# Batch 0 of a linear-attention and gated-FFN kernel: sums of phi(k) by products of their own, kv straight from the loaded v, phi of q's second part in two pieces

## The chip, the cores and the metric

The kernel runs on one core of a Trainium2 chip. The metric is the device time of one execution in microseconds (us). The kernel before takes 297.05 us (median of three runs, 296.93 to 297.34). A verdict of faster or slower needs 2%, which is 5.9 us here; the change is far smaller than that, so most of this document is about where a saved microsecond went, read from traces. All results compared are of fast runs (a run is called slow when it lies over 1.5% above the fastest of its kernel).

Engines: PE multiplies matrices (PEld is its weight load), DVE and ACT work elementwise, POOL issues most loads, SP the stores.

## The reference, cut to what matters

```python
def phi(x): return np.where(x > 0, x, np.exp(x) - 1.0) + 1.0
q_p, k_p = phi(q), phi(k)                        # 8 batches, 8 heads, 576 tokens, 64 wide
kv  = np.einsum('bhsd,bhse->bhde', k_p, v)
z   = np.sum(k_p, axis=2)                        # the "sums"
num = np.einsum('bhsd,bhde->bhse', q_p, kv)
den = np.einsum('bhsd,bhd->bhs', q_p, z)[..., None] + 1e-06
x   = (num / den)  # -> [4608, 512]
h   = x @ w_in                                   # 512 -> 2048
out = (h * sigmoid(beta * h)) @ w_out            # 2048 -> 512
```

## The kernel before: the parts that matter

PE works batch by batch: h of batch b, then y of batch b, with the attention of batch b+1 between the y products. Batch 0 has nothing to hide behind: its k, q, v must land, phi, kv, numerator, division and transpose run in a chain, and only then can the first h product start. "The plan" of a phase is the list of such work put between its products. While PE would idle there, `warm(n)` issues n filler products of 512 columns whose result nobody reads.

In kv, a column of ones beside v gives the sums of phi(k). So v is first copied by DVE into a wider tile, in two halves of the heads:

```python
    load_nine(v9, v, h1=2)
    load_nine(v9, v, h0=2)
...
    def v_copy0(h0, h1):
        nc.vector.tensor_copy(
            va9[:, :, h0:h1, 0:D].rearrange("p j h d -> p h j d"), v9[:, h0:h1])

    def kv_mm0(a, kvp):
        for j in range(N9):
            for g in range(2):
                ... nc.tensor.matmul(kvp[g][:, m0 : m0 + 2 * (D + 1)],
                    st["p0"][1][gs, j, 2 * a : 2 * a + 2, :],
                    va9[gs, j, 2 * a : 2 * a + 2, 0 : D + 1],
                    start=(j == 0), stop=(j == N9 - 1), skip_group_check=True)
```

The loads are issued by POOL in this order, and land one after another: k, q, v of batch 0, four blocks of w_in, two of w_out's four blocks, k and q of batch 1, w_out's third block, **v of batch 1**, w_out's last block. After the h phase of batch 0, y starts, and after ten of its sixteen blocks PE does batch 1's kv:

```python
    exp_(1, 1); exp_(1, 0); silu_table()
    relu(1, 1); relu(1, 0); w_out_scale(2)
    phi(1, 1)
    v_copy(1)          # DVE waits for v of batch 1
    phi(1, 0)
    y_phase_wide(0, {
        ...
        9: [F(kv_mm, 1), F(kv_evac, 1), F(w_out_scale, 3)],
        10: [F(q_trans, 1, 0, 1, wide=True), F(q_trans, 1, 2, 3, wide=True)],
```

Of the kernel before, what the change touches and what calls it, by code (L numbers as in the profile page):

```python
# [10 lines left out]
BF16 = mybir.dt.bfloat16  # L11
# [5 lines left out]
def kernel(  # L17
# [10 lines left out]
    nc = tc.nc  # L28

    B, H, S, D = q.shape  # L30
    DM = H * D
    DFF = moe_w_in.shape[1]
    P = 128
# [4 lines left out]
    TAIL = S - MAIN  # L38
    NT = NJ + 1
    EA = D + 2  # L40
# [5 lines left out]
    consts = ctx.enter_context(tc.tile_pool(name="consts", bufs=1))  # L46
# [4 lines left out]
    def mm_bank(shape, dtype=F32):  # L51
        return mmps.tile(shape, dtype, tag="mm", name="mm")

    def att_banks(dtype=F32):

        n = 512 if dtype == F32 else 1024
        return attps.tile([P, 2, n], dtype, tag="att", name="att")

    NX = 3
    HH = H // 2  # L60
    xqk = [consts.tile([P, 2, H, NT, D], BF16, name=f"xqk{i}") for i in range(NX)]
    vraw = [consts.tile([P, H, NT, D], BF16, name=f"vraw{i}") for i in range(2)]
    vaug = [consts.tile([P, NT, H, EA], BF16, name=f"vaug{i}") for i in range(2)]
# [51 lines left out]
    N9 = S // TAIL  # L115

    def nine(a, spec):

        names = " ".join(spec)
        flat = a.rearrange("p a b c -> p (a b c)")  # L120
        size = {"h": HH, "j": N9, "d": EA if a is vaug[0] else D}
        n = size["h"] * size["j"] * size["d"]
        return flat[:, 0:n].rearrange(f"p ({names}) -> p {names}", **size)

    q9 = nine(xqk[0][:, 0], "hjd")
    k9 = nine(xqk[0][:, 1], "hjd")
    v9 = nine(vraw[0], "hjd")
    va9 = nine(vaug[0], "jhd")

    def load_nine(dst, src, h0=0, h1=HH, j0=0, j1=N9):  # L130
        for g in range(2):
            nc.gpsimd.dma_start(  # L132
                out=dst[g * TAIL : (g + 1) * TAIL, h0:h1, j0:j1, :].rearrange(
                    "p h j d -> p h (j d)"
                ),
                in_=src[0, g * HH + h0 : g * HH + h1, :, :]
                .rearrange("h (p j) d -> p h j d", j=N9)[:, :, j0:j1, :]
                .rearrange("p h j d -> p h (j d)"),
            )
# [13 lines left out]
    load_nine(q9, q, j1=4)  # L153
    make_identity(nc, identity)
    make_identity(nc, ident16)
    load_nine(v9, v, h1=2)
    load_nine(v9, v, h0=2)
    load_nine(q9, q, j0=4)
    for i in range(4):
        nc.gpsimd.dma_start(out=w_in_sb[i], in_=w_in_v[:, :, i * 512 : (i + 1) * 512])  # L160
# [15 lines left out]
    def set_ones(i):  # L176
        nc.vector.memset(vaug[i][:, :, :, D : D + 2], 1.0)
        nc.vector.memset(vaug[i][TAIL:P, NJ, :, D : D + 2], 0.0)

    nc.vector.memset(va9[:, :, :, D : D + 2], 1.0)  # L180
    set_ones(1)



# [31 lines left out]
    st = {}  # L216

    def by_dma(b):
        return b >= DMA_T
# [48 lines left out]
    def phi0(a, j0, j1):  # L268
        nc.vector.tensor_tensor(
            st["p0"][a][:, j0:j1], st["r0", a][:, j0:j1], st["e0", a][:, j0:j1], ALU.min  # L270
        )

    def q_trans0(t, banks, c0):


        for jj in range(2 if t < NJ else 1):
            for a in range(2):
                for g in range(2):
                    gs = slice(g * TAIL, (g + 1) * TAIL)
                    m0 = c0 + a * P + jj * TAIL  # L280
                    nc.tensor.matmul(
                        banks[:, g, m0 : m0 + TAIL],
                        st["p0"][0][gs, 2 * t + jj, 2 * a : 2 * a + 2, :],
                        identity[gs, gs],
                        is_transpose=True, start=True, stop=True, skip_group_check=True,
                    )

    def q_out0(t, banks, c0, dve):
        n = rows(t)
        src = banks[:, :, c0 : c0 + 2 * P].rearrange("p g (a n) -> p g a n", a=2)  # L290
        dst = st[0, "qT"][:, t].rearrange("p (g a) n -> p g a n", g=2)
        copy(dst[:, :, :, :n], src[:, :, :, :n], dve)

    def v_copy0(h0, h1):
        nc.vector.tensor_copy(
            va9[:, :, h0:h1, 0:D].rearrange("p j h d -> p h j d"), v9[:, h0:h1]
        )

    def kv_mm0(a, kvp):
        for j in range(N9):  # L300
            for g in range(2):
                gs = slice(g * TAIL, (g + 1) * TAIL)
                m0 = a * 2 * (D + 1)
                nc.tensor.matmul(
                    kvp[g][:, m0 : m0 + 2 * (D + 1)],
                    st["p0"][1][gs, j, 2 * a : 2 * a + 2, :],
                    va9[gs, j, 2 * a : 2 * a + 2, 0 : D + 1],
                    start=(j == 0), stop=(j == N9 - 1), skip_group_check=True,
                )

    def kv_evac0(kvp):
        for g in range(2):
            for i in range(2):
                gs = slice(i * D, (i + 1) * D)
                copy(
                    kv_bd[0][g][gs, :, i, :],
                    kvp[g][gs, 0 : 4 * (D + 1)].rearrange(
                        "p (a i e) -> p a i e", a=2, i=2
                    )[:, :, i, :],
                    g == 0,  # L320
                )
# [32 lines left out]
    def rows(t):  # L354
        return P if t < NJ else TAIL
# [7 lines left out]
    def copy(dst, src, dve):  # L363
        if dve:
            nc.vector.tensor_copy(dst, src)  # L365
        else:
            nc.scalar.activation(dst, src, ACTF.Copy)
# [33 lines left out]
    def num_norm(b, t):  # L401
        n = rows(t)
        den = work.tile([P, 2, 4], F32, tag="den", name="den")
        rden = work.tile([P, 2, 4], F32, tag="rden", name="rden")
        xs = work.tile([P, 2, 4, D], BF16, tag="xs", name="xs", bufs=4)
        st[b, "xs", t] = xs
        nv = st[b, "n", t][:n, :, 0 : 4 * (D + 1)].rearrange("p a (h e) -> p a h e", h=4)
        nc.vector.tensor_scalar(den[:n], nv[:, :, :, D], 1e-6, None, ALU.add)  # L408
        nc.vector.reciprocal(rden[:n], den[:n])  # L409
        nc.vector.tensor_mul(  # L410
            xs[:n], nv[:, :, :, 0:D], rden[:n, :, :, None].to_broadcast([n, 2, 4, D])
        )
        if by_dma(b):
            nc.sync.dma_start_transpose(
                out=x_dst(b, t), in_=xs.rearrange("p a h d -> p (a h d)")[:n]
            )

    def x_dst(b, t):
        if t < NJ:
            return xT[b % 3][:, t]  # L420
        return xT_tail[:, :, b * TAIL : (b + 1) * TAIL]

    def x_trans(b, t, wide=False, dve=False):
        n = rows(t)
        xv = st[b, "xs", t].rearrange("p a h d -> p (a h d)")
        tp = tr_bank(wide)[:, 0 : KC * P].rearrange("p (c n) -> p c n", c=KC)
        for p in range(KC):
            nc.tensor.matmul(
                tp[:, p, :n], xv[:n, p * P : (p + 1) * P], identity[:n, :n],
                is_transpose=True, start=True, stop=True, skip_group_check=True,  # L430
            )
        copy(x_dst(b, t), tp[:, :, :n], dve)
# [132 lines left out]
    def warm(n):  # L565
        for _ in range(n):
            nc.tensor.matmul(  # L567
                st["warm"], g_sb[0][:, FC - 1, 0:P], g_sb[0][:, FC - 1, :],
                start=True, stop=True, skip_group_check=True,
            )  # L570

    def silu_table():
        nc.scalar.activation(small[:, 1:2], small[:, 0:1], ACTF.Silu)

    def F(f, *a, **k):
        return lambda: f(*a, **k)
# [17 lines left out]
    relu0(0, 0, 4)  # L594
    phi0(1, 5, N9)
    phi0(0, 0, 4)
    v_copy0(0, 2)
    qb = att_banks(BF16)
    q_trans0(0, qb, 0)
    q_trans0(1, qb, 256)  # L600
    kvp = [mm_bank([P, 512]) for _ in range(2)]
    kv_mm0(0, kvp)
    q_out0(0, qb, 0, False)
    q_out0(1, qb, 256, False)
    warm(1)
    v_copy0(2, HH)
    kv_mm0(1, kvp)
    kv_evac0(kvp)
    st["warm"] = mm_bank([P, 512])
    warm(1)  # L610
# [3 lines left out]
    relu0(0, 4, N9)  # L614
    silu_table()
    num_norm(0, 0)
    warm(4)
    x_trans(0, 0, dve=True)
    phi0(0, 4, N9)
    num_norm(0, 1)  # L620


    def q_tail0():
        qb3 = att_banks(BF16)
        q_trans0(4, qb3, 0)
        q_out0(4, qb3, 0, True)

    load_w_out(2)
    load_v(1)
    load_w_out(3)  # L630

    def tidy0():
        set_ones(0)
        clear_tail(0)
        nc.vector.memset(vraw[0][TAIL:P, :, NJ, :], 0.0)

    def q_second():
        qb2 = att_banks(BF16)
        q_trans0(2, qb2, 0)
        q_trans0(3, qb2, 256)  # L640
        q_out0(2, qb2, 0, False)
        st["qb2"] = qb2

    h_phase(
        0, xT[0],
# [1 line left out]
        + [(ff, 0, 2) for ff in range(4, 8)] + [(ff, 2, 4) for ff in range(8)]  # L647
        + [(ff, 0, 4) for ff in range(8, 12)],
        {
            1: [F(q_second)],  # L650
            3: [F(x_trans, 0, 1, dve=True), F(num_mm, 0, 2), F(num_norm, 0, 2),
                lambda: q_out0(3, st["qb2"], 256, False)],
            5: [F(num_mm, 0, 3), F(num_norm, 0, 3)],
            6: [F(q_tail0)],
            7: [F(x_trans, 0, 2)],
            9: [F(x_trans, 0, 3)],
            10: [F(num_mm, 0, 4), F(num_norm, 0, 4), F(tidy0)],
            14: [F(x_trans, 0, 4)],
            17: [F(w_out_scale, 0), F(w_out_scale, 1)],
        },  # L660
    )
# [114 lines left out]
```

## Time and profile before

| place in the trace before | us |
|---|---|
| kv's products of batch 0 end | 13.50 |
| first block of w_in has landed (the weight load that waited for it) | 16.37 |
| first h product | 16.77 |
| first y product | 34.27 |
| copy of batch 1's v, start and end | 41.90, 42.91 |
| batch 1's kv products start | 43.00 |
| last copy of the result | 291.44 |

The page's first line gives the busy times of the engines. PE idles 10.7 us in all, and 4.7 us of them lie in the first 20 us (busy 15.3 there) and 3.9 us after its last product (291.41 of 295.27).

```profile
PE 284.6 (96%) x1876; PEld 144.7 (49%) x1897; DVE 126.1 (43%) x267; ACT 175.0 (59%) x232; POOL 52.8 (18%) x72
```

A row of a timeline reads: start, length, engine, line of the program, operation, output and inputs, shape, how many; in brackets how long the engine stood idle before it and what ended that.

### The profile page before, as it was taken

How to read it: one execution, taken by the hardware profiler on the slowest of the kernel's cores; microseconds unless marked ns; L12 is line 12 of the kernel's file. 1: busy time of each engine (PE TensorE's matmuls, PEld its weight loads, DVE VectorE, ACT ScalarE, POOL GpSimd, SP SyncE). 2: the span in 40 equal slices, each digit the busy share in tenths (PEclk: the TensorE clock that was granted, in tenths of full speed). 3: DMA queues.
4: the chain of work that ended last, by engine and by line, in shares of the span. 5: the costliest groups of instructions: out<-in, count | busy, mean ns of one | idle time of the engine just before them, and what ended most of it. 6: DMA issues, size and time to landing. Idle time of an engine off the chain costs nothing.

```text
span 295.3 us, 4721 instructions
## 1 busy us (share of the span) xinstructions
PE 284.6 (96%) x1876; PEld 144.7 (49%) x1897; DVE 126.1 (43%) x267; ACT 175.0 (59%) x232; POOL 52.8 (18%) x72
## 2 busy tenths in 40 slices
PE   8689999999999999999999999999999999999994
PEld 3467445644555544445444544454445444444443
DVE  4776488504772174616461646154715400110012
ACT  2788786889988780778087907790770077018500
POOL 8925575444006000330020000000000000000000
PEclk9999999999999999999999999999999999999999
DMA  7999999999939933798357355024502400020033
GB/s 106 190 207 344 256 273 192 256 194 190 162 140 154 178 93 98 133 175 149 98 125 82 80 109 125 2 71 115 124 2 72 118 36 0 36 94 15 0 72 72
DMA packets 69206, 36.43 MB, mean 123 GB/s; under 512 B 37808, under 2 KB 63680, under 8 KB 69184
## 3 DMA queue, kind: packets, MB, share of 16 engines
q0 software_dynamic: 38400, 20.45, 47.5%
q1 hardware_dynamic: 30624, 15.55, 20.5%
q8 instruction: 15, 0.25, 0.3%
q10 hardware_dynamic: 160, 0.13, 0.2%
q14 instruction: 7, 0.06, 0.1%
HBM read 36.71 MB, written 9.44 MB: 156 GB/s over the span
## 4 chain that ended last, share of the span: by engine, by line
PE 72%; DMA 14%; POOL 5%; ACT 4%; issue 3%; DVE 1%; POOLq 0%; ACTq 0%; DVEq 0%
PE mm L500 33%; PE mm L448 33%; DMA vraw<-in_v_dram 9%; DMA xT<-in_moe_w_out_dram 5%; PE att L394 3%; ACT e L228 2%; POOL xqk L132 1%; PE att L339 1%; PE mm L532 1%; POOL w_in L160 1%; ACT L228 1%; POOL vraw L132 1%; POOL vraw L72 1%; ACT g L440 1%; DVE qk_p L241 0%
## 5 line engine op out<-in xcount | busy, mean ns | idle before, releaser
L440 ACT ACTIVATE g<-mm,beta_c 128x512 bf16<-128x512 f32 (+2 forms) x156 | 97.4, 632 | 88.4 <-PE mm L448 88.2
L500 PE MATMUL mm<-w_out,g 128*128 128x512 bf16 x541 | 127.2, 379 | 1.2 <-issue 0.3
L448 PE MATMUL mm<-xT,w_in 128*128 128x512 bf16 (+2 forms) x560 | 108.0, 349 | 0.8 <-DVE xT L365 0.8
L448 PEld LDWEIGHTS <-w_in 128*128 128x128 bf16 x656 | 62.1, 98 | 61.7 <-issue 0.7
L500 PEld LDWEIGHTS <-g 128*128 128x128 bf16 x560 | 52.8, 98 | 57.3
L510 DVE COPY y_sb<-mm 128x512 f32<-128x512 f32 x27 | 18.7, 691 | 70.6 <-PE mm L500 68.4
L228 ACT ACTIVATE e<-xqk 128x2560 bf16<-128x2560 bf16 x14 | 31.9, 2329 | 0.1
L410 DVE TENSOR_TENSOR xs<-att,rden 128x512 bf16<-128x512 f32 (+1 forms) x40 | 27.6, 689 | 1.4
L241 DVE TENSOR_TENSOR qk_p<-r,e 128x2560 bf16<-128x2560 bf16 x14 | 20.8, 1489 | 13.1 <-ACT e L228 12.4
L350 DVE CAST kv_bd<-att 64x130 bf16<-64x130 f32 x28 | 8.2, 292 | 34.5 <-PE att L339 34.1
L72 POOL DMA_DIRECT2D vraw<-in_v_dram x7 | 6.4, 910 | 75.6 <-DVE vaug L365 71.0
L408 DVE TENSOR_SCALAR den<-att 128x8 f32<-128x8 f32 (+1 forms) x40 | 6.4, 161 | 26.9 <-PE att L394 26.7
L394 PEld LDWEIGHTS <-q_pT 128*128 128x128 bf16 (+1 forms) x160 | 11.7, 100 | 10.4 <-DVE xs L410 2.1
L394 PE MATMUL att<-kv_bd,q_pT 128*128 128x130 bf16 (+1 forms) x160 | 15.8, 221 | 0.6 <-DVE kv_bd L365 0.3
L448 PE MATMUL mm<-xT_tail,w_in 128*128 128x512 bf16 x63 | 13.9, 379 | 0.1
L236 DVE TENSOR_SCALAR r<-xqk 128x2560 bf16<-128x2560 bf16 x14 | 11.6, 830 | 3.8 <-DMA xqk<-in_q_dram 2.3
L567 PE MATMUL mm<-g 128*128 128x512 bf16 x35 | 9.9, 436 | 1.2 <-DVE g L144 1.2
L228 ACT ACT_TABLE_LOAD x7 | 9.0, 1283 | 0.1
L72 POOL DMA_DIRECT2D xqk<-in_k_dram x7 | 6.9, 981 | 11.1 <-ACT e L228 4.6
L409 DVE RECIPROCAL rden<-den 128x8 f32<-128x8 f32 (+1 forms) x40 | 8.1, 201 | 1.4
L72 POOL DMA_DIRECT2D xqk<-in_q_dram x7 | 6.5, 922 | 6.6 <-DMA xqk<-in_k_dram 2.5
L76 POOL DMA_DIRECT2D xqk<-in_k_dram x7 | 7.0, 1000 | 2.6 <-DMA w_in<-in_moe_w_in_dram 2.6
(72 smaller groups left out, 141.7 us busy)
## 6 DMA issues: line engine op xcount, KB each, us to landing
out_dram<-y_sb SPq DMA_DIRECT2D x28, 256.0 KB, 2.3
xqk<-in_k_dram POOLq DMA_DIRECT2D x7, 512.0 KB, 10.7
xqk<-in_q_dram POOLq DMA_DIRECT2D x7, 512.0 KB, 11.3
vraw<-in_v_dram POOLq DMA_DIRECT2D x7, 512.0 KB, 11.7
w_in<-in_moe_w_in_dram POOLq DMA_DIRECT2D x4, 512.0 KB, 11.4
g<-in_moe_w_out_dram POOLq DMA_DIRECT2D x4, 512.0 KB, 10.9
out_dram<-y_sb SPq DMA_DIRECT2D x14, 128.0 KB, 5.2
xqk<-in_moe_w_out_dram POOLq DMA_DIRECT2D x2, 512.0 KB, 14.5
```

What stands on the lines that cost most here:

```text
L72: eng.dma_start(out=dst[:, :, 0:NJ, :].rearrange("p h j d -> p h (j d)"), in_=src[b, :, 0:MAIN, :].rearrange("h (p j) d -> p h (j d)", j=NJ),)
L228: nc.scalar.activation(st[b, "e", a][:, h0:h1], xqk[b % NX][:, a, h0:h1], ACTF.Exp)
L236: nc.vector.tensor_scalar(st[b, "r", a][:, h0:h1], xqk[b % NX][:, a, h0:h1], 0.0, 1.0, ALU.max, ALU.add)
L241: nc.vector.tensor_tensor(st[b, "p"][:, a].rearrange("p j (h d) -> p h j d", h=H)[:, h0:h1], st[b, "r", a][:, h0:h1], st[b, "e", a][:, h0: ...
L350: nc.vector.tensor_copy(kv_bd[b % 2][i][gs, :, g, :], st[b, "kvp"][gs, 2 * i : 2 * i + 2, :])
L394: nc.tensor.matmul(nps[:n, p // 2, c0 : c0 + 2 * (D + 1)], st[b, "qT"][:, t, p, :n], kv_bd[b % 2][p // 2][:, p % 2], start=True, stop=True ...
L410: nc.vector.tensor_mul(xs[:n], nv[:, :, :, 0:D], rden[:n, :, :, None].to_broadcast([n, 2, 4, D]))
L440: nc.scalar.activation(g_sb[b % 2][:, ff, c0:c1], hp[:, c0:c1], ACTF.Silu, scale=beta_c[:, ff : ff + 1],)
L448: nc.tensor.matmul(hp[:, c0:c1], w_in_sb[ff // 4][:, kc, (ff % 4) * P : (ff % 4 + 1) * P], x[:, t0:t1, kc, :] if b < B else x[:, kc, c0:c1 ...
L500: nc.tensor.matmul(yp, g_sb[b % 2][:, ff, t * P : (t + 1) * P], w_out_sb[ff // 4][:, ff % 4, :], start=(ff == 0), stop=(ff == FC - 1),)
L510: nc.vector.tensor_copy(y_sb, yp)
L567: nc.tensor.matmul(st["warm"], g_sb[0][:, FC - 1, 0:P], g_sb[0][:, FC - 1, :], start=True, stop=True, skip_group_check=True,)
```

## The change

Its intent: take the copies of v off the chain that leads to the first h product, compute the sums while PE waits, and give the q path of the later token tiles smaller pieces. Its core (cuts marked):

```diff
-    load_nine(v9, v, h1=2)
-    load_nine(v9, v, h0=2)
+    load_nine(v9, v, j1=6)
+    load_nine(v9, v, j0=6)
...
+    ones = consts.tile([P, 2], BF16)
+    nc.vector.memset(ones, 1.0)
...
+    def kv_mm0(kvp, j0, j1, of_v):
+        for j in range(j0, j1):
+            for a in range(2):
+                for g in range(2):
+                    gs = slice(g * TAIL, (g + 1) * TAIL)
+                    cols = kv_cols(kvp, g, a)
+                    nc.tensor.matmul(
+                        cols[:, :, 0:D] if of_v else cols[:, :, D],
+                        st["p0"][1][gs, j, 2 * a : 2 * a + 2, :],
+                        v9[gs, 2 * a : 2 * a + 2, j, :] if of_v else ones[gs],
+                        start=(j == 0 and a == 0 and not of_v), ...
...
-    v_copy0(0, 2)
+    kvp = [mm_bank([P, 512]) for _ in range(2)]
+    kv_mm0(kvp, 0, N9, False)
     ... q_trans0, q_out0 ...
-    warm(1)
-    v_copy0(2, HH)
-    kv_mm0(1, kvp)
+    kv_mm0(kvp, 0, 6, True)
+    kv_mm0(kvp, 6, N9, True)
...
     num_norm(0, 0)
+    phi0(0, 4, 6)
     warm(4)
     x_trans(0, 0, dve=True)
-    phi0(0, 4, N9)
+    qb2 = att_banks(BF16)
+    q_trans0(2, qb2, 0)
+    q_out0(2, qb2, 0, False)
     num_norm(0, 1)
+    phi0(0, 6, N9)
...  # the plan of the h phase: q's transposes earlier and together,
     # the second x copy and q's last copy on ACT, tile 4's numerator sooner
```

More of the change, by code (lines that the diff above doesn't have):

```diff
@@ L120, in nine @@
         flat = a.rearrange("p a b c -> p (a b c)")
-        size = {"h": HH, "j": N9, "d": EA if a is vaug[0] else D}
+        size = {"h": HH, "j": N9, "d": D}
         n = size["h"] * size["j"] * size["d"]
@@ L127 @@
     v9 = nine(vraw[0], "hjd")
-    va9 = nine(vaug[0], "jhd")
     def load_nine(dst, src, h0=0, h1=HH, j0=0, j1=N9):
@@ L178, in set_ones @@
         nc.vector.memset(vaug[i][TAIL:P, NJ, :, D : D + 2], 0.0)
-    nc.vector.memset(va9[:, :, :, D : D + 2], 1.0)
-    set_ones(1)
+    for i in range(2):
+        set_ones(i)
+    ones = consts.tile([P, 2], BF16)
+    nc.vector.memset(ones, 1.0)
     beta_c = consts.tile([P, FC], F32)
@@ L292, in q_out0, with kv_cols @@
         copy(dst[:, :, :, :n], src[:, :, :, :n], dve)
-    def v_copy0(h0, h1):
-        nc.vector.tensor_copy(
-            va9[:, :, h0:h1, 0:D].rearrange("p j h d -> p h j d"), v9[:, h0:h1]
-        )
-    def kv_mm0(a, kvp):
-        for j in range(N9):
-            for g in range(2):
-                gs = slice(g * TAIL, (g + 1) * TAIL)
-                m0 = a * 2 * (D + 1)
-                nc.tensor.matmul(
-                    kvp[g][:, m0 : m0 + 2 * (D + 1)],
-                    st["p0"][1][gs, j, 2 * a : 2 * a + 2, :],
-                    va9[gs, j, 2 * a : 2 * a + 2, 0 : D + 1],
-                    start=(j == 0), stop=(j == N9 - 1), skip_group_check=True,
-                )
+    def kv_cols(kvp, g, a):
+        m0 = a * 2 * (D + 1)
+        return kvp[g][:, m0 : m0 + 2 * (D + 1)].rearrange("p (i e) -> p i e", i=2)
+    def kv_mm0(kvp, j0, j1, of_v):
[8 more added lines that the diff above has]
+                        v9[gs, 2 * a : 2 * a + 2, j, :] if of_v else ones[gs],
+                        start=(j == 0 and a == 0 and not of_v),
+                        stop=(j == N9 - 1 and a == 1 and of_v),
+                        skip_group_check=True,
+                    )
     def kv_evac0(kvp):
@@ L600 @@
     q_trans0(1, qb, 256)
-    kvp = [mm_bank([P, 512]) for _ in range(2)]
-    kv_mm0(0, kvp)
     q_out0(0, qb, 0, False)
     q_out0(1, qb, 256, False)
-    warm(1)
-    v_copy0(2, HH)
-    kv_mm0(1, kvp)
+    kv_mm0(kvp, 0, 6, True)
+    kv_mm0(kvp, 6, N9, True)
     kv_evac0(kvp)
@@ L616 @@
     num_norm(0, 0)
+    phi0(0, 4, 6)
     warm(4)
     x_trans(0, 0, dve=True)
-    phi0(0, 4, N9)
+    qb2 = att_banks(BF16)
+    q_trans0(2, qb2, 0)
+    q_out0(2, qb2, 0, False)
     num_norm(0, 1)
-    def q_tail0():
-        qb3 = att_banks(BF16)
-        q_trans0(4, qb3, 0)
-        q_out0(4, qb3, 0, True)
+    phi0(0, 6, N9)
     load_w_out(2)
@@ L632, in tidy0, with q_rest0 @@
     def tidy0():
-        set_ones(0)
         clear_tail(0)
         nc.vector.memset(vraw[0][TAIL:P, :, NJ, :], 0.0)
-    def q_second():
-        qb2 = att_banks(BF16)
-        q_trans0(2, qb2, 0)
+    def q_rest0():
         q_trans0(3, qb2, 256)
-        q_out0(2, qb2, 0, False)
-        st["qb2"] = qb2
+        q_trans0(4, qb2, 512)
+        q_out0(3, qb2, 256, False)
+        q_out0(4, qb2, 512, False)
     h_phase(
@@ L649 @@
         {
-            1: [F(q_second)],
-            3: [F(x_trans, 0, 1, dve=True), F(num_mm, 0, 2), F(num_norm, 0, 2),
-                lambda: q_out0(3, st["qb2"], 256, False)],
+            3: [F(x_trans, 0, 1), F(num_mm, 0, 2), F(num_norm, 0, 2), F(q_rest0)],
             5: [F(num_mm, 0, 3), F(num_norm, 0, 3)],
-            6: [F(q_tail0)],
             7: [F(x_trans, 0, 2)],
-            9: [F(x_trans, 0, 3)],
-            10: [F(num_mm, 0, 4), F(num_norm, 0, 4), F(tidy0)],
-            14: [F(x_trans, 0, 4)],
+            8: [F(num_mm, 0, 4), F(num_norm, 0, 4)],
+            9: [F(x_trans, 0, 3), F(tidy0)],
+            12: [F(x_trans, 0, 4)],
             17: [F(w_out_scale, 0), F(w_out_scale, 1)],
```

## The prediction

> **What bounds the kernel now.** I read the page's engine totals first: PE is busy 284.6 of 295.3 us, so only 10.7 us of PE idle exist, and 72% of the chain that ended last is PE. The change touches batch 0 alone, that is the opening. So I read the opening in the views by time, asking which wait ends last and whether a saved microsecond can reach the end.
>
> The page's slices (40 of 7.4 us each) show two regimes: PE at 8 or 9 tenths from the second slice on, and the DMA engines at 9 through the first ten slices.
>
> ```profile
> PE   8689999999999999999999999999999999999994
> DMA  7999999999939933798357355024502400020033
> ```
>
> The timeline of the opening, by engine, shows where PE stands still. The columns are start, length, engine, line and operation, and in brackets the idle time and what ended it.
>
> ```profile
> 11.14 0.41 PE L281 MATMUL att<-identity,qk_p 64*128 64x64 bf16 x16 [1.33 <-DVE qk_p L269]
> 11.51 0.69 PE L304 MATMUL mm<-vaug,qk_p 64*128 64x130 bf16 x18
> 12.81 0.69 PE L304 MATMUL mm<-vaug,qk_p 64*128 64x130 bf16 x18 [0.61 <-DVE vaug L295]
> 16.77 0.61 PE L448 MATMUL mm<-xT,w_in 128*128 128x128 bf16 x8 [0.52 <-DVE xT L365]
> ```
>
> The second half of kv waits for a copy of v (third line), and the first h product starts at 16.77. But PE's weight loads of the same stretch, and DVE's copy of v, say what stands behind:
>
> ```profile
> 16.37 0.10 PEld L448 LDWEIGHTS <-w_in 128*128 128x128 bf16 x1 [0.29 <-DMA w_in<-in_moe_w_in_dram]
> 42.99 0.71 PEld L339 LDWEIGHTS <-qk_p 128*64 128x64 bf16 x40 [0.42 <-DVE vaug L365]
> 12.20 0.56 DVE L295 COPY vaug<-vraw 128x1152 bf16<-128x1152 bf16 x1 [0.74 <-DMA vraw<-in_v_dram]
> 41.90 1.01 DVE L365 COPY vaug<-vraw 128x2560 bf16<-128x2560 bf16 x1 [0.70 <-DMA vraw<-in_v_dram]
> ```
>
> The first block of w_in lands only at 16.37. And at 42.99 PE begins batch 1's kv, having waited for the copy of batch 1's v, whose load lands at about 41.85. The chain of waits in order of time says it outright: from 13.2 to 41.8 the end depends on loads alone, then on DVE, and returns to PE at 45.49.
>
> ```profile
> 13.22 15.40 DMA xT<-in_moe_w_out_dram
> 28.61 0.29 issue
> 28.90 1.09 POOL vraw L72
> 30.00 0.20 issue
> 30.19 11.62 DMA vraw<-in_v_dram
> ...
> 42.84 1.47 DVE qk_p L241
> ...
> 45.49 0.62 PE att L375 x8
> ```
>
> So the opening up to 43 us is bound by the loads, the rest by PE: all waits of PE after 40 us sum to 0.9 us.
>
> [...] the stretch 13.5 to 22.4 us, mostly 1024-byte packets, moved 207 GB/s, and 32.6 to 33.6 us, mostly 512-byte ones, 196 GB/s. [...] 18 products with 64 rows and 130 columns took 0.69 us, 38 ns each.
>
> **The change part by part.**
> *Removed:* two copies of v on DVE, 0.45 and 0.56 us. The second is on the path (v lands 12.14, copy to 12.76, kv at 12.81).
> *Added:* 36 products of two columns for the sums. They need phi(k) only, ready in two parts at 9.3 and about 10.3 us (DVE rows at 8.50 and 9.58). At no more than 38 ns each they take 1.4 us, mostly inside PE's idle stretch of 1.33 us before 11.14, where PE waits for phi(q). At worst they push the q transposes by 0.2 us; beside the path.
> *Moved:* kv is now 24 products on v's first two thirds, then 12 on the last third. The first 24 start after the transposes at about 11.5 and take 24 x 38 ns = 0.9 us, to 12.4. The last third lands where the second half did, about 12.2; 12 products more, 0.45 us, end at 12.85 instead of 13.50. **Gain 0.65 us at the eviction of kv.**
> *phi of q in two pieces:* the 128x512 piece, an estimate of 0.35 to 0.4 us scaled from 0.82 us for 128x1280, fits the 0.49 us in which DVE waits for the x transpose (row at 16.29). The other piece comes after the second token tile's division, which starts 0.8 us sooner for it.
> *At the first h product:* 0.65 us earlier would be 16.1, but w_in lands at 16.37. So it starts at about 16.45: **0.3 us of the 0.65 survive.**
> *In the h phase:* the copy of x's second tile and of q's last piece go from DVE to ACT: 0.60 + 0.38 = about 1.0 us more for ACT (rows of such copies on ACT: 128x512 in 0.60, 128x256 in 0.38), while ACT is busy 3.56 us of the 4 from 20 to 24 us and 3.98 of the 4 from 24 to 28. PE saves some of its gaps at 17.4 to 19.5 (0.28 us and 0.2 us). I work out the order on ACT by hand: four silus to about 18.1, x copy to 18.7, h of the second tile from 18.7 instead of 19.46; then two q copies and four silus to 20.8, x copy to 21.4, the next silus from 21.4 instead of 21.84. So PE reaches y of batch 0 about 0.3 us (0 to 0.6) before 34.27.
> *At batch 1's kv:* PE then arrives about 0.3 us early and **waits for the copy of v**, which ends at 42.91 and moves only with the loads. Loads: same bytes, same number of transfers; v's packets go from 512 of 1152 bytes to 512 of 768 and 512 of 384. [...] the two rates above suggest less, +0.1. The 16 engines are never idle before 42 us, so this delay adds to the landing of batch 1's v: 41.85 + 0.1.
> *Sum:* -0.65 (kv) +0.35 (w_in) -0.0 (h phase) +0.3 (wait for v) = 0, with +0.1 for packets, and 0.1 that PE may lose at 43 us now: **297.0 us**.
>
> **The rivals.**
> *A. The gain carries through* (296.3): 0.65 us of the path go and nothing takes their place. For: PE is 96% busy, and the wait removed is real. Against: the weight load at 42.99 already waits 0.42 us for v, and the chain from 13 to 42 us is all loads.
> *B. ACT becomes the bound of the h phase* (297.3 to 297.6): 1 us more on ACT at 98% busy from 24 to 28 us. Against: ACT starts this stretch sooner and loses idle gaps of 0.2 to 0.3 us each. Only a delay beyond what the early start gives would show.
> *C. Smaller packets delay the loads* (297.1 to 297.3): they are the bound, so each 0.1 us counts whole. Against: the rates of small packets above.
> *D. The transfers are hidden differently than I think* (296.6): the landing of batch 1's v varies by some tenths from run to run or with the spacing of the issues on POOL, and it alone sets the time.
>
> **Range and chances.** My main line gives 297.0; A, partly true, takes 0.5 off; B or C add up to 0.5. The three runs before spread over 0.4 us. So 296.95 us, range 296.4 to 297.5. 2% would be 5.9 us, more than half of all PE idle, which no part of this change can give or take: faster 0.01, same 0.985, slower 0.005.
>
> **What would show it.** Right: kv's products end near 12.85; the first w_in weight load has waited about 0.6 us for w_in and still starts near 16.4; kv of batch 1 starts within 0.2 us of 42.99 after a longer wait (0.6 to 0.9 us) for v's copy; the load of v still lands near 41.9. Wrong: kv of batch 1 starts at 42.5 or before (A or D: v came earlier), PE arrives there without a wait (B: then silus have delayed h), or v lands past 42.2 (C).

What is cut above: a paragraph of general rules, of which only the measured rates stay (207 and 196 GB/s, 38 ns a product), and a reckoning of v's smaller packets from a figure that no trace here shows, which gave more than 0.1 us and on which the upper end of rival C seems to lean. The sum: -0.65 + 0.35 - 0.0 + 0.3 = 0, with 0.1 for the packets and 0.1 at 43 us. Its 0.1 for the packets is the estimate from those two rates: they differ by 5%, which is 0.16 us of 3.1 us (0.59 MB of v at about 190 GB/s), taken as 0.1.

## The result, and the profile after

The changed kernel took 296.82 us (median of four runs, 296.72 to 297.06), the kernel before in the same rounds 297.13 us. Ratios here and below are the mean time of one kernel's fast runs over that of the other's of the same rounds, so not quite the ratio of the medians quoted: 0.9991, 95% interval 0.9973 to 1.0008. Nothing can be told apart by the time alone.

The page of the changed kernel, and then PE's timeline in the opening:

```profile
PE 285.1 (97%) x1911; PEld 144.9 (49%) x1932; DVE 125.2 (42%) x264; ACT 175.5 (59%) x234; POOL 52.2 (18%) x72
```

```profile
10.70 0.60 PE L307 MATMUL mm<-ones,qk_p 64*128 64x2 bf16 x36
...
11.40 1.18 PE L307 MATMUL mm<-vraw,qk_p 64*128 64x128 bf16 x36
...
15.63 0.40 PE L433 MATMUL mm<-identity,xs 128*128 128x128 bf16 x4 [0.88 <-DVE xs L415]
...
17.09 1.07 PE L453 MATMUL mm<-xT,w_in 128*128 128x128 bf16 x16 [0.84 <-DMA w_in<-in_moe_w_in_dram]
```

kv's products ran without a stop and ended at 12.58 instead of 13.50: the change saved its 0.92 us there. But the first h product started at 17.09, **0.32 us later** than before (16.77), because w_in's first block landed later. The saving went into two waits of PE, 0.88 us for the division (0.20 before) and 0.84 us for w_in (before, 0.52 us at this place for the copy of x).

Where the two kernels meet again is batch 1's kv. First the kernel before (PE, then POOL), then the changed one (PE, DVE, POOL):

```profile
34.27 8.80 PE L500 MATMUL mm<-w_out,g 128*128 128x512 bf16 x39
43.00 0.82 PE L339 MATMUL att<-vaug,qk_p 128*64 128x65 bf16 x40
...
41.41 0.88 POOL L72 DMA_DIRECT2D vraw<-in_v_dram  x1 [1.14 <-DMA vraw<-in_v_dram]
```

```profile
34.09 8.80 PE L505 MATMUL mm<-w_out,g 128*128 128x512 bf16 x39
42.82 0.82 PE L344 MATMUL att<-vaug,qk_p 128*64 128x65 bf16 x40
...
41.88 0.83 DVE L370 COPY vaug<-vraw 128x2560 bf16<-128x2560 bf16 x1 [0.94 <-DMA vraw<-in_v_dram]
...
41.88 1.30 POOL L72 DMA_DIRECT2D vraw<-in_v_dram  x1 [2.07 <-DMA vraw<-in_v_dram]
```

The load landed at the same time (the copy starts at 41.88; before, 41.90). PE came 0.18 us earlier (34.09 beside 34.27), and the copy of v happened to take 0.83 us instead of 1.01, so it also ended 0.20 us earlier. Both reasons allow kv at 42.82 instead of 43.00. The last copy of the result started at 291.23 instead of 291.44: 0.2 us is all that this pair of traces differs by.

A useful constant comes out of the traces in which PE does not wait there: from the first y product to batch 1's kv it takes 8.73 us (42.61 - 33.88 in run e7, 42.58 - 33.85 in run e10). With it, PE's own arrival in the trace before is 34.27 + 8.73 = 43.00, exactly where kv started, and in the trace after 34.09 + 8.73 = 42.82, again exactly. The copy ended 0.09 and 0.11 us ahead of that. So in these two traces PE and the copy of v were almost level, with PE the later. That is one execution each: in e2 below, the kernel before once more, the copy ended 0.62 us ahead of kv's start.

### The profile page after: what moved, and what is told of

It is laid out like the page before. It is cut to its first block, busy times and chain, and to the rows that moved or that the text cites. A ratio compares the mean times of both kernels' runs of the same rounds, so it can differ in the third digit from the quotient of the medians.

```text
span 295.1 us, 4791 instructions
## 1 busy us (share of the span) xinstructions
PE 285.1 (97%) x1911; PEld 144.9 (49%) x1932; DVE 125.2 (42%) x264; ACT 175.5 (59%) x234; POOL 52.2 (18%) x72
## 4 chain that ended last, share of the span: by engine, by line
PE 71%; DMA 17%; ACT 4%; POOL 4%; issue 3%; DVE 0%; POOLq 0%; ACTq 0%
PE mm L453 33%; PE mm L505 32%; DMA xqk<-in_q_dram 9%; DMA vraw<-in_v_dram 4%; DMA w_in<-in_moe_w_in_dram 4%; PE att L399 2%; ACT e L229 2%; POOL xqk L131 1%; PE att L344 1%; PE mm L537 1%; ACT L229 1%; POOL vraw L131 1%; ACT g L445 1%; POOL w_in L159 1%; ACT L445 0%
## 5 line engine op out<-in xcount | busy, mean ns | idle before, releaser
L72 POOL DMA_DIRECT2D xqk<-in_k_dram x7 | 8.0, 1150 | 10.2 <-ACT e L229 3.6
L256 ACT ACTIVATE e<-xqk 128x1280 bf16<-128x1280 bf16 (+1 forms) x4 | 4.4, 1154 | 5.1 <-DMA xqk<-in_k_dram 4.6
```

The costliest lines, as they stand in the source:

```text
L72: eng.dma_start(out=dst[:, :, 0:NJ, :].rearrange("p h j d -> p h (j d)"), in_=src[b, :, 0:MAIN, :].rearrange("h (p j) d -> p h (j d)", j=NJ),)
```

## The experiments

Theory: two things allow batch 1's kv, PE's arrival and the end of the copy of v, and the later of them sets the time; a gain on one alone is lost. In the opening, w_in's first block takes the place of the wait removed. Rivals: the gain carries through on PE; or ACT, with about 1 us of copies more, slows the h phase; or the loads alone bound.

The runs fall in groups (e1 to e4, e5 to e8, e9 to e11, e12), each on one chip with the kernel before beside it. Collected first, from the traces (one profiled execution each, us):

| run | kv ends | w_in there: POOL released | first h | first y | copy of v ends | kv of batch 1 |
|---|---|---|---|---|---|---|
| before | 13.50 | 16.62 | 16.77 | 34.27 | 42.91 | 43.00 |
| e2 before again | 13.50 | 16.24 | 16.80 | 34.30 | 42.41 | 43.03 |
| e4 plan alone | 13.40 | 16.30 | 16.95 | 34.09 | 42.97 | 43.03 |
| changed | 12.58 | 17.34 | 17.09 | 34.09 | 42.71 | 42.82 |
| e1 changed again | 12.34 | 16.90 | 16.65 | 33.65 | 42.45 | 42.50 |
| e3 kv alone | 12.80 | 17.27 | 17.02 | 34.09 | 43.02 | 43.07 |
| e5 v by heads | 12.11 | 16.74 | 16.50 | 33.49 | 42.41 | 42.46 |
| e6 four y products less | 12.59 | 16.94 | 16.70 | 33.69 | 42.56 | 42.61 |
| e7 one load less | 12.40 | 17.13 | 16.89 | 33.88 | 41.66 | 42.61 |
| e10 filler | 12.74 | 17.10 | 16.86 | 33.85 | 42.28 | 42.58 |
| e11 early v | 12.92 | 17.39 | 17.15 | 34.14 | 41.52 | 42.87 |

(e8 and e9, whose profiled executions ran with a halved clock, and e12 stand in their own paragraphs. The third column is when POOL, which waits for the same load, went on; it stands some 0.25 us after PE's weight load could.)

**e1, the changed kernel again.**

> The changed kernel once more, for a tighter interval and a second trace. Main theory (batch 1's kv is gated by the copy of batch 1's v, which the loads gate; the 0.18 us that the end gained is the copy taking 0.83 us beside 1.01 us, because POOL did not issue a load before it): ratio 0.999 to 1.000; kv of batch 1 starts 0.08 to 0.1 us after that copy ends; if POOL wakes before the copy starts, the copy takes about 1.0 us and the gain vanishes. Rival (the opening gained 0.2 us on PE and carried it): ratio 0.9993 and below, kv of batch 1 at 42.8 us whatever the copy does.

297.21 us (296.48 to 298.11, six runs) beside 296.82; ratio 1.0009 (0.9991 to 1.0026). With the first session's 0.9991: the same; the ratio lies just outside the 0.999 to 1.000 expected. The copy took 0.83 us although POOL had woken 0.1 us before it, so my detail about POOL's waking was too simple; kv started 0.05 us after the copy. The spread of 1.6 us, wider than before's 1.1, is the first hint of something that this theory does not hold (see e8 and e9).

**e2, the kernel before again**, one look (296.79 us; a single run, so its state is unknown).

> The kernel before once more, one look for a second trace. Main theory: kv of batch 1 starts 0.08 to 0.1 us after the copy of v ends, at 42.8 us if the copy takes 0.82 us and at 43.0 us if it takes 1.01 us. Rival (PE's own path): 43.0 us whatever the copy takes. The first block of w_in lands at 16.4 us if that belongs to this kernel, anywhere from 16.3 to 17.1 if it is chance.

A miss for the part on the copy: the copy took 1.08 us but ended at 42.41, since the load landed 0.57 us sooner than in the first trace. kv started at 43.03 = 34.30 + 8.73, when PE arrived. So the landing of v moves by half a microsecond from execution to execution, and the later of the two gates decides.

**e3, kv alone** on the kernel before: the load order of v, the sums, no copy; phi and plan as before.

> Only the kv part on the kernel before (sums by own products, v straight from the load in two token parts, no copy), phi of q and the plan of the h phase as before. Main theory: kv's products end near 12.6 us beside 13.5, the first h product waits for w_in, kv of batch 1 starts within 0.2 us of 42.9; ratio 0.999 to 1.0005. Rival (the 0.9 us of kv carry through): ratio 0.997. If the token parts of v delay w_in, w_in lands at 17.0 here and in e1 and at 16.4 in e2 and e4.

297.12 us beside 296.82; ratio 1.0014 (0.9998 to 1.003), above the 1.0005 expected. kv's products ended 0.7 us sooner than before and nothing came of it: w_in made PE's weight load wait 1.45 us,

```profile
17.02 0.45 PEld L453 LDWEIGHTS <-w_in 128*128 128x128 bf16 x8 [1.45 <-DMA w_in<-in_moe_w_in_dram]
```

and kv of batch 1 started at 43.07, 0.05 us after a copy that ended late. The rival "0.9 us carry through" falls.

**e4, phi's pieces and the plan alone**, kv with its copies.

> Only phi of q in two pieces and the new plan of the h phase on the kernel before, kv with its copies of v as before. Main theory: y of batch 0 starts within 0.3 us of 34.2, kv of batch 1 within 0.2 us of 42.9; ratio 0.999 to 1.001. Rival (ACT, with 1 us of copies more, becomes the bound of the h phase): y of batch 0 at 34.5 us or later, PE arrives after the copy of v has ended, ratio 1.001 or more.

296.73 us beside 296.82; ratio 1.0 (0.9982 to 1.0018). From the first h product to the first y product it takes 17.14 us instead of 17.50, so 0.36 us less with the new plan, and ACT's added copies do not slow it: that rival falls. But e3, with the old plan, took 17.07 us (34.09 - 17.02): the stretch got as short with the old plan and a first h product that started later. How much of the 0.36 us is the plan's is therefore not shown; in both runs y starts at 34.09, 0.18 us sooner than before. kv of batch 1 waited for its copy (42.97), and the gain was lost there.

**e5, v in head parts**, all else as changed.

```diff
-    load_nine(v9, v, j1=6)
-    load_nine(v9, v, j0=6)
+    load_nine(v9, v, h1=2)
+    load_nine(v9, v, h0=2)
...  # kv_mm0: the v products head pair by head pair
```

> The changed kernel with v loaded in two head parts as before (512 packets of 1152 bytes) and kv's v products in the same order, the rest of the change kept. Theory (the token parts' smaller packets make one DMA engine late, and so the first block of w_in land at 16.6 to 17.1 beside 16.1 to 16.4): w_in lands at 16.4 us or before, kv's products end at 12.6 to 12.9, the first h product starts at 16.2 to 16.6, y of batch 0 at 33.2 to 33.6; kv of batch 1 then waits for the copy of v until 42.4 to 42.9, so the ratio is 0.998 to 1.000. Rival (w_in's landing is chance): w_in at 16.6 to 17.1 here too.

297.05 us beside 297.0; ratio 0.9996 (0.9981 to 1.0012). w_in landed at 16.50, just outside what I had expected, and in e10 and e11, which keep the head parts, at 16.85 and 17.14. So smaller packets of v are **not** enough to explain why w_in is late; that theory falls (nor does any view used here show a single late DMA engine). What the table does show: POOL's release by w_in comes at 16.24 to 16.62 us in the three traces with the copies of v, and at 16.74 or later in the eight listed without. e3 and e4 tie it to the kv part. Why, is open; the total moved is no answer: by 16 us it was 2.44 MB before (released at 16.62) and 2.45 MB in the changed kernel (17.34).

**e6, four y products less** (wrong result): block 5 of batch 0's y is skipped, ahead of batch 1's kv.

```diff
             for t in range(4):
+                if b == 0 and ff == 5:
+                    continue
                 y_mm(b, yp[t], t, ff)
```

> The changed kernel without the four y products of one block of columns in batch 0 (wrong result on purpose): 4 x 0.2155 = 0.86 us less on PE right ahead of batch 1's kv. Theory (kv of batch 1 starts at the later of PE's arrival and the copy of v): PE arrives at 41.5 to 42.0, kv starts at the copy's end plus 0.1, 42.4 to 42.8, PE waits 0.6 to 1.0 us there, gain 0 to 0.35 us: ratio 0.9985 to 1.000. Rival (PE alone bounds, the load's landing is hidden): kv at 41.9, ratio 0.997.

296.88 us beside 297.0; ratio 0.9998 (0.9982 to 1.0013). 0.86 us of PE's work were gone and nothing was gained. PE's timeline and then DVE's show why:

```profile
33.69 7.93 PE L505 MATMUL mm<-w_out,g 128*128 128x512 bf16 x36
42.61 0.82 PE L344 MATMUL att<-vaug,qk_p 128*64 128x65 bf16 x40 [0.99 <-DVE vaug L370]
...
41.73 0.83 DVE L370 COPY vaug<-vraw 128x2560 bf16<-128x2560 bf16 x1 [0.43 <-DMA vraw<-in_v_dram]
```

The whole saving stands in the bracket: PE waited 0.99 us for the copy of v, and that for its load.

**e7, one load less** (wrong result): half of w_out's second block is not loaded, its other half is used twice.

```diff
-        [xT_f[1], xT_f[2]],
+        [xT_f[1], xT_f[1]],
...
-        for ii in range(2):
+        for ii in range(1 if i == 1 else 2):
```

> The changed kernel with one load of 0.5 MB of w_out left out ahead of batch 1's v (other data in its place, wrong result on purpose): at the 400 GB/s of such loads 1.3 us less. Theory: the copy of v ends 1.0 to 1.3 us sooner, at 41.2 to 41.7; kv of batch 1 starts when PE arrives, 42.4 to 42.8, and PE's second wait for kv's eviction (0.22 to 0.28 us) goes: ratio 0.998 to 0.9995. Rival (the loads alone bound): 1.2 us gained, ratio 0.996.

296.69 us beside 297.0; ratio 1.0003 (0.9983 to 1.0023). PE's timeline and DVE's:

```profile
33.88 8.80 PE L505 MATMUL mm<-w_out,g 128*128 128x512 bf16 x40
42.61 0.82 PE L344 MATMUL att<-vaug,qk_p 128*64 128x65 bf16 x40
...
40.83 0.83 DVE L370 COPY vaug<-vraw 128x2560 bf16<-128x2560 bf16 x1 [0.31 <-DMA vraw<-in_v_dram]
```

The copy ended 1.05 us sooner than in the changed kernel (41.66), and kv started when PE arrived: 33.88 + 8.73 = 42.61. The rival "loads alone" falls as "PE alone" did. PE's weight load of this kv, in the changed kernel and then here, shows the same wait of 0.42 us, although here the copy had long ended:

```profile
42.81 0.71 PEld L344 LDWEIGHTS <-qk_p 128*64 128x64 bf16 x40 [0.42 <-DVE vaug L370]
...
42.61 0.71 PEld L344 LDWEIGHTS <-qk_p 128*64 128x64 bf16 x40 [0.42 <-issue]
```

**e8, both edits** (wrong result).

> Both edits of the two runs before at once (wrong result on purpose). Theory of two bounds side by side: kv of batch 1 starts at 41.5 to 42.0, gain 0.8 to 1.1 us, more than the sum of the two alone (0 to 0.35 and 0.15 to 0.6): ratio 0.996 to 0.9975. Rival (PE alone): the same gain as without the y products alone, so ratio 0.997 in both. Rival (loads alone): the same as with the load left out alone.

295.52 us beside 297.0; ratio 0.9965 (0.9945 to 0.9986). Four of six executions took 295.48 to 295.53, some 1.5 us less than before; each edit alone gave nothing that could be measured. Setting executions with a low clock aside in all three, the means lie 0.05 us (e6), 0.44 (e7) and 1.48 (e8) below the kernel before (296.98): both together gave far more than the sum. So there are two gates side by side. But two executions took 296.81 and 297.02, and the profiled one was the latter: there the h phase lasted 17.92 us instead of 17.0. A table of two stretches (columns: PE, PEld, DVE, ACT, POOL busy, granted PE clock, DMA share, GB/s) shows the cause:

```profile
14.79:18.20 3.41, 1.52 (x28) 1.30 (x29) 2.78 (x7) 2.56 (x6) 0.68 (x2) 1.00 1.24 206
18.20:21.62 3.42, 3.42 (x43) 2.98 (x40) 1.43 (x5) 2.65 (x8) 0.92 (x2) 0.50 1.24 207
```

PE's clock was granted at 0.50 for 3.41 us, right after a stretch of the same length in which PE was busy for 1.52 us only. The wait for w_in that the change opened lies in that stretch (1.24 us, to 17.30), and the one for the division (0.74 us, to 15.44) reaches into it. That gave a new theory: the change lets the clock drop in some executions.

**e9, the filler taken out.** The four filler products stand where the change opened the first wait.

```diff
     phi0(0, 4, 6)
-    warm(4)
     x_trans(0, 0, dve=True)
```

> The changed kernel without the four filler products that PE runs while it waits for the first tile's division (0.86 us of work with no use for the result; the result stays right). Theory ([...] 1.52 us of 3.41 in the one trace that shows a halving[...]): PE's busy time in that stretch falls to 0.9 to 1.3 us, the clock drops in most executions, and h of batch 0 is 1 to 1.5 us late: median 297.5 to 298.3, ratio 1.003 to 1.005. Rival (PE only waits there for w_in, the filler is worth nothing): the same time as the changed kernel, ratio 0.999 to 1.001.

298.05 us beside 296.84; ratio 1.0038 (1.0019 to 1.0057). Removing work that nobody uses cost over 1 us. The mean clock of all six executions was 0.987 to 0.994. The profiled one had the clock at half for 6.83 us:

```profile
12.13:15.54 3.41, 1.75 (x31) 1.08 (x27) 2.58 (x7) 3.23 (x6) 2.21 (x4) 1.00 1.25 206
15.54:18.95 3.41, 2.43 (x29) 2.28 (x29) 1.86 (x5) 2.42 (x7) 0.90 (x1) 0.50 1.24 205
18.95:22.37 3.42, 3.42 (x41) 2.98 (x39) 1.80 (x6) 2.57 (x7) 1.24 (x2) 0.50 1.24 206
```

The changed kernel's first trace had a stretch of 1.76 us busy, and its clock stayed up:

```profile
13.61:17.03 3.42, 1.76 (x21) 0.81 (x18) 2.94 (x9) 3.23 (x4) 1.19 (x2) 1.00 1.25 208
```

Busy time alone gives no rule. PE was busy for 1.52 us (e8) and 1.75 us (here) in the 3.41 us before the drop, with waits of up to 1.24 and 1.30 us among them; but 1.76 us in the changed kernel, and 1.47 us in the kernel before (9.40 to 12.81), were followed by full clock. Why the clock drops in one execution and not in another is not shown. Products take longer at half the clock (the first sixteen h products 1.89 us here, 1.07 in the changed kernel), and after the 2.43 us of the second row it stayed at half.

Half the clock for one stretch of 3.41 us takes 0.0058 off a mean over 295 us, so an execution with a drop shows 0.994 or less. Counting these over all executions whose clock is listed:

| kernel | executions | with a mean clock of 0.994 or less |
|---|---|---|
| before (the rounds beside e1 to e12) | 34 | 0 |
| e4 plan alone | 6 | 0 |
| changed (first session and e1) | 10 | 2 |
| e3, e5, e6, e7, e8 (kv part, no more filler) | 28 | 7 |
| e9 filler out | 6 | 6 |
| e10, e11, e12 (more filler) | 14 | 0 |

In e7 the two low ones took 297.47 and 298.06 us, the four others 296.28 to 296.79: 1.2 us between the means. The same difference is 1.4 us in e8, 0.8 in e1 and e3 and 0.2 in e5, so a drop costs some 0.2 to 1.4 us. The two of e1 took 297.28 and 298.11, but two others of e1 at full clock took 297.14 and 297.33: the clock is not the only thing that spreads the times. This is a cost of the change that my prediction did not have at all. It seems to come from the kv part (2 of 6 executions of e3, none of 6 of e4), though the counts are small.

**e10, more filler**, with v in head parts.

```diff
     phi0(0, 4, 6)
-    warm(4)
+    warm(7)
     x_trans(0, 0, dve=True)
     qb2 = att_banks(BF16)
     q_trans0(2, qb2, 0)
+    warm(2)
```

> v in head parts as in e5 and five filler products more where PE waits (three before the x transpose, two before the first h product). Theory of the clock: [...] no execution has the halved clock, so the upper values (297.1 to 298.1 in the kernels of this kind so far) go: median 296.4 to 296.7, ratio 0.998 to 0.9995. First h product at 16.4 to 16.7. Rival (the upper values come from elsewhere): the same spread as e5, 296.5 to 297.3.

296.53 us (296.40 to 296.68) beside 296.84; ratio 0.999 (0.9978 to 1.0002). The upper values are gone, and no execution had a low clock, as expected: PE was busy 3.08 and 2.92 us in the two stretches from 12.70 to 19.52. That the clock alone made the upper values is not shown: e5, the same loads of v without the filler, had 297.26 and 297.10 at full clock and 297.05 at a low one.

```profile
12.70:16.11 3.41, 3.08 (x30) 1.56 (x30) 2.63 (x8) 2.85 (x4) 1.88 (x3) 1.00 1.25 207
16.11:19.52 3.41, 2.92 (x48) 2.17 (x46) 2.73 (x8) 3.28 (x11) 1.08 (x2) 1.00 1.24 207
```

**e11, e10 with batch 1's v loaded earlier**: ahead of the second half of w_out's third block, whose scaling goes to ACT.

```diff
-    load_w_out(2)
+    load_w_out(2, (0,))
     load_v(1)
+    load_w_out(2, (1,))
     load_w_out(3)
...
     exp_(1, 0)
+    w_out_scale(2, False, (2, 3))     # on ACT
     silu_table()
...
-    w_out_scale(2)
+    w_out_scale(2, True, (0, 1))
```

> As e10, and batch 1's v loaded ahead of the second half of w_out's third block (whose scaling goes to ACT), as a version that may beat both. Theory of two bounds at batch 1's kv: the copy of v ends 1 us sooner, at 41.2 to 41.6, PE arrives at 42.2 to 42.4 and starts kv without a wait, the wait for kv's eviction (0.28 us) goes: 0.3 to 0.6 us below e10, median 295.9 to 296.3, ratio 0.9965 to 0.998. Rival (w_out's late half, or ACT with two products more, becomes the new wait): y of batch 0 stops at its block 10 for 0.3 us or more, and the time is that of e10.

296.74 us beside 296.84; ratio 0.9992 (0.9979 to 1.0005). The copy ended at 41.52 as expected, and PE did not wait for it. But in this execution w_in landed at 17.14, so PE arrived only at 42.87. The gate of the loads is open; the other one, w_in, keeps PE back. A miss in time, by a gate that I had named for the opening and left in place.

**e12, e11 with w_in's first block in two halves**, the version that should beat both.

```diff
-    for i in range(4):
-        nc.gpsimd.dma_start(out=w_in_sb[i], in_=w_in_v[:, :, i * 512 : (i + 1) * 512])
+    for c0, c1 in ((0, 256), (256, 512), (512, 1024), (1024, 1536), (1536, 2048)):
+        i = c0 // 512
+        nc.gpsimd.dma_start(
+            out=w_in_sb[i][:, :, c0 - 512 * i : c1 - 512 * i], in_=w_in_v[:, :, c0:c1])
...
-    warm(2)
+    warm(1)
```

> As e11, with the first block of w_in loaded in two halves of 256 columns (the first two h products need the first half only) and one filler product fewer ahead of the first h product. Theory (after the change the landing of w_in's first block sets the first h product, and from there 17.0 us of h and 8.73 us of y lead to batch 1's kv): the first half lands at 15.6 to 16.1, so the first h product starts when x is copied, 16.3 to 16.6, beside 17.15 in e11; y of batch 0 at 33.3 to 33.6, kv of batch 1 at 42.0 to 42.4 without a wait for v: median 296.0 to 296.3, ratio 0.9965 to 0.9985. Rival (the late engine delays the half as it does the whole, or the second half then stops the third h product): the first h products as in e11, ratio 0.999 to 1.000.

296.21 us (295.97 to 296.53, four runs) beside 296.90; ratio 0.9978 (0.9964 to 0.9993), correct, and the first version here with the right result whose interval lies wholly below the kernel before: 0.2%, far under the 2%. It stacks four edits on the changed kernel; only their sum is measured. PE's timeline:

```profile
16.26 0.61 PE L456 MATMUL mm<-xT,w_in 128*128 128x128 bf16 x8
17.23 0.62 PE L456 MATMUL mm<-xT,w_in 128*128 128x128 bf16 x8 [0.36 <-DMA w_in<-in_moe_w_in_dram]
...
33.78 8.80 PE L508 MATMUL mm<-w_out,g 128*128 128x512 bf16 x40
42.50 0.82 PE L347 MATMUL att<-vaug,qk_p 128*64 128x65 bf16 x40
```

The first h product starts as soon as x is ready, at 16.26. The third one then waits for the second half, which lands at 17.23: half of my rival came true (no view shows the late engine of its other half), and y starts at 33.78, not at 33.3 to 33.6.

## Why the prediction was right or wrong

**The time: right** (296.95 predicted, 296.82 measured, the same), and so was the core of the reasoning: the 0.65 us at kv would not reach the end. e3, e6, e7 and e8 show that. But two of the signs that the prediction set for itself failed (the w_in weight load near 16.4, a longer wait for v at kv), and PE reached batch 1's kv without a wait, which it had listed as a sign of being wrong. That the number came out is partly luck: the first h product was 0.64 us later than forecast (17.09 beside 16.45) and the h phase 0.50 us shorter, and these two nearly cancel. The last sum is also unclear: 0, with 0.1 and 0.1 more, on 297.05 would be 297.25, not 297.0. By its steps:

- **kv's products.** Predicted end 12.85; 12.58 and 12.34 measured. The sums took 0.60 us, not up to 1.4, and v had landed by the time that PE needed it.
- **w_in takes over.** The mechanism was right, the size was not. I took w_in's landing (16.37) as fixed by the loads ahead of it, and gave the first h product 16.45. It started at 17.09 and 16.65. In the traces without the copies of v the block lands later; the term "0.3 us of the 0.65 survive" measured -0.32 us in the first trace and +0.12 us in e1. The cause of the later landing is open.
- **The h phase.** I gave it nothing. It shortened from 17.50 to 17.00 us (from first h to first y). It took 17.14 us with the new plan alone (e4) and 17.07 with the kv part alone (e3), so the two do not add up, and part of it only makes up for the later start. ACT's added copies, rival B, did no harm.
- **PE waits for batch 1's v.** The gate is real (e6: 0.99 us of waiting for 0.86 us of work removed). But the step "kv of batch 1 starts after a longer wait, 0.6 to 0.9 us" failed: PE did not arrive early enough to wait at all. With the first h product later by 0.32 us and the h phase shorter by 0.50 us it came 0.18 us sooner, 0.11 us after the copy of v had ended.
- **The weight load's wait of 0.42 us for v**, my main evidence against rival A, was misread. The same 0.42 us stand in the changed kernel at 42.81, and in e7 too, where the copy had ended 0.95 us before. In the trace before, PE's products ran on to 43.07 while its weight load waited; 34.27 + 8.73 = 43.00 says that PE arrived just then. The load was a second gate, level with PE, not one ahead of it.
- **Smaller packets (rival C).** No delay is seen: the copy of batch 1's v started at 41.88 instead of 41.90. But this start moved from 41.33 to 41.90 between two executions of the kernel before, so the 0.1 us that was forecast cannot be told from one pair.
- **Where the 0.2 us of the trace come from.** Partly from rival D: the copy of v took 0.83 us instead of 1.01. In the three traces with copies in batch 0 POOL began a load 0.4 to 0.5 us before this copy, and the copy took 1.01 to 1.09 us instead of 0.82; in the seven traces (changed, e1, e3, e5, e6, e7, e10) where POOL began at most 0.2 us ahead of it, it took 0.83 us and POOL's issue 1.30 to 1.48 instead of 0.88. Where POOL began first, the copy grew by the overlap of the two records less 0.2 us: by 0.19, 0.26 and 0.27 for overlaps of 0.39, 0.46 and 0.47, and by nothing for overlaps of 0.15 to 0.18 (e8, e9, e12). Where the copy held, in the seven traces and in e11, POOL's issue ended 0.47 to 0.48 us after the copy did. An estimate from these records: what does not run beside the copy is POOL's issue from about 0.40 us after its start (0.88 us alone, less the 0.48 us left after the copy) to 0.20 us before its end. Why, is not shown. No run changed this alone, so it is read from traces and not shown by an experiment.
- **What was missing.** The clock. Waits that cost nothing by the timeline let PE's clock drop in 2 of the changed kernel's 10 executions, for about 0.8 us (e1's means). e9 and e10 show the drop, by taking filler away (6 of 6 executions) and by adding it (none of 5).

## What to carry to other kernels

Before you count a gain, ask at each place where two chains meet who else must be there: here one load and one engine were level within 0.1 us in the first traces, each the later one in some executions, and neither gain alone could show. A weight load that waits is no proof that its engine waits; compare the engine's own arrival with the event. And when a change turns work into waiting on the matrix engine, look at the clock that it was granted (0.50 for 3.41 us in e8's trace and for 6.83 us in e9's): filler that "does nothing" was worth about 1 us here (e9: 0.38% of 297 us, against the kernel before).
